# Attention values with the probabilities as the stationary operand in six of 32 head pairs, and a rank product with the last tokens on 128 rows

## The chip, the cores and the metric

The kernel runs on one core of a Trainium2 chip. The metric is the device time of one execution, in microseconds. The core has TensorE (matrix products, PE in the profile; its weight loads are a line of their own, PEld), VectorE (DVE), ScalarE (ACT), GpSimd (POOL) and SyncE (SP), which here issues the DMAs. Products go to PSUM, here in tiles of 512 float32 columns (a bank) on 128 partitions; all other data live in SBUF, on 128 partitions too.

## The reference

Eight batches, eight heads, 576 tokens, head width 64, all in float32. Causal attention with a decay is followed by a low-rank mix of the tokens and a two-layer network over the channels.

```python
def _attn_ref(q, k, v, f):
    scores = (1 / np.sqrt(D)) * np.matmul(q, k.transpose(0, 1, 3, 2))
    cum = np.cumsum(np.log(np.clip(f, 0.0001, 1.0)), axis=-1)
    scores = np.where(causal, -1e9, scores + cum[:, :, :, None] - cum[:, :, None, :])
    attn = np.exp(scores - np.max(scores, axis=-1, keepdims=True))
    attn = attn / (np.sum(attn, axis=-1, keepdims=True) + 1e-09)
    return np.matmul(attn, v)                     # 8 x 8 x 576 x 64

def _moe_ref(x, U, V, w_ch1, w_ch2):              # x: 8 x 576 x 512, heads side by side
    h = x.transpose(0, 2, 1) @ U @ V              # U 576 x 32, V 32 x 576
    u = x + h.transpose(0, 2, 1)
    return u + np.maximum(u @ w_ch1, 0.0) @ w_ch2 # 512 -> 2048 -> 512
```

## The kernel before, in words

**Tiling.** The work of attention is cut into 32 pairs of heads (`p`, four to a batch, `NP`), the 576 tokens into four chunks of 128 (`NM`, `MAIN` = 512) and a tail of 64 (`TAIL`). In most products float32 numbers are split into a high and a low part of the type float32r, and the product is made of three (or two) such products. The first six pairs (`p < NF`) instead use plain float32 operands in the score and value products; the profile shows each plain float32 product as two weight loads and two matmuls.

**Order.** `step(t)` is written out by hand for TensorE: ten slots (`s`), in which three pairs are in work at once. Pair `p = SEQ[t]` gets its scores, pair `a = SEQ[t-1]` has its probabilities turned and its first head's values made, pair `c = SEQ[t-2]` gets its second head's values, its turned result and its rank product. `SEQ` has an empty place after the fourth pair. `defer(phase, fn)` puts the ACT and DVE work that follows a product into the next slot, sorted by phase; `at(phase, fn)` does the same in the present slot. TensorE's order is as written (and SP's too in the first step and from the eighth on); that of the other engines comes from the framework's planner. In free places of the slots, and in steps of their own kind (`mix_units`), the mix and the first `NA` = 6 of 16 hidden chunks of the network run for batches that are done. After the attention, a sweep over the tokens makes the other ten chunks; it takes roughly the last 500 us and the change does not touch it.

**Probabilities and values.** A score product `score(p, j, i)` leaves rows of 128 queries; `P[j][i]` holds their exponentials, 128 queries by up to 512 keys. The 64 tail queries of both heads share one tile, `ptl`. `turn_p` and `turn_tail` turn 128 by 128 blocks with TensorE (`T`, `T_v`), and ScalarE copies them to `PTh` (for `p >= NF` VectorE makes the low part `PTl`), with one run of columns for each key chunk, at `OC`. `turn_small` turns the last 64 key columns of the tail queries to `PT4`. `values_direct` (`p < NF`) then makes the values transposed: the 128 columns of `vr` (both heads' values, a chunk of keys) are the stationary operand and up to 448 columns of `PTh` pass; half of the output rows belong to the other head and are not used. ScalarE copies the head's own 64 rows to `xT`, `turn_x` turns four blocks of `xT` back and `turn_small` the last 64 tokens, and VectorE multiplies them with the reciprocal sums `rv` into `xn`, the batch's activations.

**Rank product.** `split_x` splits a pair's 128 columns of `xn` into `xh` (ACT) and `xl` (POOL), and `ranks` multiplies them with `Us` (U's high and low parts side by side, 64 columns): four token chunks of 128 rows, and then two products on the 64 rows of the tail.

**Buffers.** `psV` has one buffer of two banks, which `T_v`, the turned tail, and both value products of a pair take in turn; `psT` has two buffers of one bank.

The helper that splits a tile:

```python
def split(dh, dl, src, heng, leng):     # heng copies to dh, leng writes src - dh to dl
```

Of the kernel before, what the change touches and what calls it, by code (L numbers as in the profile page):

```python
# [8 lines left out]
F32 = mybir.dt.float32  # L9
F32R = mybir.dt.float32r  # L10
# [3 lines left out]
ALU = mybir.AluOpType  # L14
# [7 lines left out]
P = 128  # L22
NHP = H // 2
NM = 4
# [7 lines left out]
MASKED = -8.0e9  # L32
OC = (0, 576, 1024, 1344)
PTW = 1536
NG = B + 1
NX = 3
NF = 6
# [3 lines left out]
def tile_decay_attention_moe(ctx, tc, qk, v, f, U, V, w1, w2, out):  # L41
# [6 lines left out]
    def words(ap):  # L48
        return ap.bitcast(I32)
# [140 lines left out]
    def load_w(u):  # L190
        if u in staged or u >= len(UNITS):
            return
        kind, fc = UNITS[u]
        n = {"U": (NM + 1) * RK, "V": S}.get(kind, 512)
        if kind == "w2":

            spare = xn[NX - 1].rearrange("p c d -> p (c d)").bitcast(I32)
            if fc % 2:
                raw, a = spare[:, 1536:2560], sb.tile([P, 512], I32, tag="w2a", name=f"stg{u}")
            else:  # L200
                raw, a = spare[:, 0:1024], spare[:, 1024:1536]
        else:
            t = sf.tile([P, 3 * S], I32, tag=("uh", "ul", "hh", "hl")[u % 4], name=f"stg{u}")
            raw, a = t[:, 0 : 2 * n], t[:, 2 * n : 3 * n]
        staged[u] = raw.rearrange("p (n t) -> p n t", t=2), a
        if kind == "w1":
            nc.sync.dma_start(raw, w1_src(fc))
        elif kind == "w2":
            tc.keep_in_program_order(nc.sync.dma_start(raw, w2_src(fc)))
        elif kind == "V":  # L210
            for g in range(4):
                nc.sync.dma_start(raw[32 * g : 32 * g + 32], words(V))
        else:
            r4 = raw.rearrange("p (c r) -> p c r", c=NM + 1)
            nc.gpsimd.memset(r4[64:128, NM], 0)
            nc.sync.dma_start(r4[:, 0:NM], words(U[0:MAIN]).rearrange("(c p) r -> p c r", p=P))
            nc.sync.dma_start(r4[0:64, NM], words(U[MAIN:S]))

    def decode_w(u):
        load_w(u)  # L220
# [70 lines left out]
    def make_vs(p):  # L291
        if p < NF:
            return
        vr = st[p]["vr"]
        VS = sb.tile([P, NM + 1, 2, P], F32R, tag="VS", name=f"VS{p}")
        st[p]["VS"] = VS
        for j in range(2):
            vh = VS[:, :, j, 64 * j : 64 * j + 64]
            vl = VS[:, :, j, 64 * (1 - j) : 64 * (1 - j) + 64]
            nc.scalar.copy(vh, vr[:, :, j])  # L300
            nc.gpsimd.tensor_tensor(vl, vr[:, :, j], vh.bitcast(F32), op=ALU.subtract)

    def copy(eng, dst, src, keep):
        i = eng.copy(dst, src) if eng is nc.scalar else eng.tensor_copy(dst, src)  # L304
# [104 lines left out]
    def inverse(p):  # L409
        z = st[p]  # L410
        sm = z["sm"]
        z["rv"] = sb3.tile([P, 10], F32, tag="rv", name=f"rv{p}")
        nc.vector.tensor_tensor(sm[:, 8:9], sm[:, 8:9], sm[:, 9:10], op=ALU.add)
        nc.vector.tensor_scalar(sm[:, 0:9], sm[:, 0:9], 1e-9, None, op0=ALU.add)
        nc.vector.reciprocal(z["rv"][:, 0:9], sm[:, 0:9])
        nc.vector.tensor_copy(z["rv"][0:64, 9:10], z["rv"][64:128, 8:9])

    def evac(dsth, dstl, src):
        defer(0, lambda: nc.scalar.copy(dsth, src))  # L419
        if dstl is None:  # L420
            return
        defer(2, lambda: nc.vector.tensor_tensor(dstl, src, dsth.bitcast(F32), op=ALU.subtract))  # L422
# [3 lines left out]
    def turn_p(p, j, g):  # L426
        z = st[p]
        if "PTh" not in z and p < NF:
            z["PTh"] = sb.tile([P, 2, PTW], F32, tag=("PTh", "PTl")[p % 2], name=f"PTh{p}")
            z["PT4"] = sb.tile([P, P], F32, tag="PT4", name=f"PT4{p}")  # L430
        elif "PTh" not in z:
            z["PTh"] = sb.tile([P, 2, PTW], F32R, tag="PTh", name=f"PTh{p}")
            z["PTl"] = sb.tile([P, 2, PTW], F32R, tag="PTl", name=f"PTl{p}")
            z["PT4"] = sb.tile([P, P], F32R, tag="PT4", name=f"PT4{p}")
        grp = GRP[g]
        if (j, g) == (0, 2):
            z["tv"] = psV.tile([P, 1024], F32, tag="V", name=f"T{p}_v")
            tp = z["tv"][:, 0:512]
        else:
            tp = psT.tile([P, 512], F32, tag="T", name=f"T{p}_{j}{g}")  # L440
        for x, (c, i) in enumerate(grp):
            nc.tensor.transpose(tp[:, P * x : P * x + P], z["P"][j][i][:, P * c : P * c + P], ident)  # L442

        x = 0
        for c in sorted({c for c, _ in grp}):
            m = sum(1 for cc, _ in grp if cc == c)
            sl = slice(OC[c], OC[c] + P * m)
            evac(z["PTh"][:, j, sl], z["PTl"][:, j, sl] if p >= NF else None, tp[:, P * x : P * (x + m)])
            x += m

    def turn_tail(p):
        z = st[p]
        tp = z["tv"][:, 512:1024]
        for c in range(NM):
            nc.tensor.transpose(tp[:, P * c : P * c + P], z["ptl"][:, P * c : P * c + P], ident)

        tpv = tp.rearrange("p (c j t) -> p j c t", c=NM, j=2)
        for c in range(0, NM, 2):
            o = [(OC[c + y] + MAIN - P * (c + y)) // TAIL for y in range(2)]
            pair = [  # L460
                z[n].rearrange("p j (y d) -> p j y d", d=TAIL)[:, :, o[0] : o[1] + 1 : o[1] - o[0]]
                for n in ("PTh", "PTl")
                if n in z
            ]
            evac(pair[0], pair[1] if p >= NF else None, tpv[:, :, c : c + 2])

    def turn_small(pa, px):

# [28 lines left out]

    X0 = 384

    def values_direct(p, j):  # L500


        z = st[p]
        if j == 0:
            z["xT"] = sb.tile([P, S], F32, tag="xT", name=f"xT{p}")
        vr, xT, pt = z["vr"].rearrange("p c j d -> p c (j d)"), z["xT"], z["PTh"]
        pv = psV.tile([P, 1024], F32, tag="V", name=f"V{p}_{j}")
        nc.tensor.matmul(pv[:, X0:512], vr[:, 0], pt[:, j, 0:P], start=True, stop=True)
        for c in range(NM):
            lo = max(P * c, P)  # L510
            nc.tensor.matmul(  # L511
                pv[:, X0 + lo : X0 + S], vr[:, c], pt[:, j, OC[c] + lo - P * c : OC[c] + S - P * c],
                start=c == 0, stop=False,
            )
        nc.tensor.matmul(
            pv[:, X0 + MAIN : X0 + S], vr[0:64, NM], z["PT4"][0:64, 64 * j : 64 * j + 64], start=False, stop=True
        )
        defer(1, lambda: nc.scalar.copy(xT[OWN[j]], pv[OWN[j], X0 : X0 + S]))

    def values(p, j):  # L520
        if p < NF:
# [41 lines left out]
    def split_x(p):  # L563
        z = st[p]
        X = xn[z["b"] % NX]
        fs = slice(P * z["hp"], P * z["hp"] + P)
        z["xh"] = sb.tile([P, NM + 1, P], F32R, tag="xh", name=f"xh{p}")
        z["xl"] = sb.tile([P, NM + 1, P], F32R, tag="xl", name=f"xl{p}")
        split(z["xh"], z["xl"], X[:, :, fs], nc.scalar, nc.gpsimd if p < NP - 1 else nc.vector)

    TSb = {}

    def ranks(p):
        z = st[p]
        b, hp = z["b"], z["hp"]
        if hp == 0:
            TSb[b] = sf.tile([P, DM], F32R, tag="TS", name=f"TS{b}")
        TS = TSb[b]
        fs = slice(P * hp, P * hp + P)
        tp = psT.tile([P, 512], F32, tag="T", name=f"Tt{p}")  # L580
        for i in range(NM + 1):
            kk = P if i < NM else TAIL
            for x, xx in enumerate((z["xh"], z["xl"])):
                nc.tensor.matmul(  # L584
                    tp[0:64, 0:P], Us[0:kk, i], xx[0:kk, i], start=i == 0 and x == 0, stop=i == NM and x == 1
                )


        defer(1, lambda: nc.scalar.copy(TS[0:64, fs], tp[0:64, 0:P]))
        defer(1, lambda: nc.scalar.copy(TS[96:128, fs], tp[0:32, 0:P]))  # L590
        defer(
            4,
            lambda: nc.vector.tensor_tensor(
                TS[64:96, fs], tp[0:32, 0:P], TS.bitcast(F32)[0:32, fs], op=ALU.subtract
            ),
        )
# [164 lines left out]
    def step(t):  # L761
# [11 lines left out]
        for s in range(6 + 2 if last else SLOTS):  # L773
# [9 lines left out]
                clear_operands()  # L783
            if s == 3 and pa:
                at(4, lambda: make_vs(a))
            if s == 9 and pa:
                at(4, lambda: inverse(a))
            if s == 6 and NF <= nxt_p < NP:
                at(5, lambda: parts(p + 1, 0, ENGINES))
# [28 lines left out]
                values(c, 1)  # L818
            if pa and s < 3:
                turn_p(a, 0, s)  # L820
            if px and s == (2 if last else 3):
                turn_x(c)
            if s == (3 if last else 4) and (pa or px):
                turn_small(a if pa else None, c if px else None)
            if pa and s == 5:
                turn_tail(a)
            if pa and 6 <= s < 9:
                turn_p(a, 1, s - 6)
            if pa and s == 7:
                values(a, 0)  # L830
            if px and s == (6 if last else 8):
                ranks(c)

# [344 lines left out]
```

## Time and profile before

| | |
|---|---|
| median of three runs | 1281.25 us (1280.5 to 1281.74) |
| the profiled execution | 1281.79 us, of which the span of its instructions is 1280.0 us |
| PE busy / PEld busy | 1237.0 us / 1081.7 us |
| DVE / ACT / POOL busy | 882.6 us / 654.2 us / 323.1 us |
| mean granted TensorE clock | 0.993 |

Busy times are of spans that overlap for TensorE: a matmul's span goes on while the next has begun, so what a product costs is read from start to start. A form such as `128*64 128x128` is the part of the array that is used (rows by columns) and the shape that passes. The pages cut the span into 40 slices of 32 us; the first six pairs lie between 11 us and about 170 us.

### The profile page before, as it was taken

Reading aid. Unit: us, or ns where it says so; the run is one execution under the profiler, and the core shown is the slowest. Engines: PE = TensorE matmul, PEld = TensorE weight load, DVE = VectorE, ACT = ScalarE, POOL = GpSimd, SP = SyncE. Lnnn points to the kernel's source line nnn. Section 1 sums busy time; section 2 is a strip of 40 time slices with the busy share of each in tenths; the row PEclk is TensorE's granted clock in tenths of the full one; section 3 lists DMA queues with packets and bytes.
Section 4 is the critical chain, followed back from the end, with each engine's and each line's share of the span. In section 5 each row is a group of like instructions: output and inputs, shape, how many; then the busy total and the mean of one; then the engine's idle time right before and its main releaser. Section 6 shows DMA issues by size and latency. Waiting matters only on the chain.

```text
span 1280.0 us, 21478 instructions
## 1 busy us (share of the span) xinstructions
PE 1237.0 (97%) x7644; PEld 1081.7 (85%) x7644; DVE 882.6 (69%) x2247; ACT 654.2 (51%) x1779; POOL 323.1 (25%) x306
## 2 busy tenths in 40 slices
PE   5998999999999999999999989999999999999998
PEld 3766788998998998989988878888888888888887
DVE  6666578877778668678677599985655646556453
ACT  5676777866777667778657444332122221212221
POOL 4453544444444434444433100000000000000000
PEclk9997999999999999999999999999999999999999
DMA  7334333532533524335323156110311303113010
GB/s 203 104 97 131 81 94 86 159 104 58 160 95 99 153 67 139 106 87 159 85 76 105 67 181 244 61 67 8 125 72 61 132 4 129 67 66 129 4 34 33
DMA packets 67466, 125.85 MB, mean 98 GB/s; under 512 B 7280, under 2 KB 31856, under 8 KB 65312
## 3 DMA queue, kind: packets, MB, share of 16 engines
q1 hardware_dynamic: 67232, 124.48, 31.4%
q8 instruction: 60, 0.98, 0.3%
q14 instruction: 46, 0.38, 0.1%
q10 hardware_dynamic: 128, 0.01, 0.0%
HBM read 88.67 MB, written 35.78 MB: 97 GB/s over the span
## 4 chain that ended last, share of the span: by engine, by line
PE 82%; DVE 8%; ACT 3%; issue 3%; DMA 2%; POOL 1%; SPq 0%; ACTq 0%; DVEq 0%; POOLq 0%
PE O L960 17%; PE M L1036 14%; PE A L677 10%; PE B L695 10%; PE V L534 5%; PE T L442 4%; PE S L344 3%; PE S L341 2%; PE S L345 2%; PE V L511 2%; PE Hb L946 2%; PE Tt L584 2%; DMA u<-ud 1%; PE Tx L552 1%; DVE xn L1019 1%
## 5 line engine op out<-in xcount | busy, mean ns | idle before, releaser
L1059 DVE TENSOR_TENSOR sum<-M,sum 128x256 f32<-128x256 f32 x280 | 117.7, 423 | 162.8 <-PE M L1036 159.9
L937 ACT ACTIVATE bh<-sum 128x256 fp32r<-128x256 f32 x160 | 66.3, 418 | 250.4 <-DVE sum L1059 250.4
L365 DVE CUSTOM_DVE_ANT_0 S<-S,mask 128x128 f32<-128x128 f32 (+3 forms) x256 | 126.2, 497 | 92.4 <-PE S L345 65.9
L373 ACT ACTIVATE P<-S,nm 128x128 f32<-128x128 f32 (+3 forms) x256 | 136.7, 535 | 58.7 <-DVE nm L365 57.0
L960 PE MATMUL O<-b2h,bh 128*128 128x512 f32 x360 | 143.2, 398 | 0.0
L960 PE MATMUL O<-b2l,bh 128*128 128x512 f32 x360 | 142.6, 396 | 0.0
L960 PE MATMUL O<-b2h,bl 128*128 128x512 f32 x360 | 142.0, 395 | 0.0
L677 PE MATMUL A<-uh,w1h 128*128 128x256 f32 (+1 forms) x384 | 121.1, 315 | 1.4 <-DVE hl L681 1.4
L677 PE MATMUL A<-ul,w1h 128*128 128x256 f32 (+1 forms) x384 | 113.5, 295 | 0.0
L677 PE MATMUL A<-uh,w1l 128*128 128x256 f32 (+1 forms) x384 | 113.4, 295 | 0.0
L304 POOL CAST G<-qk 64x576 fp32r<-64x576 f32 x52 | 34.3, 660 | 272.5 <-PE St L345 152.7
L695 PE MATMUL B<-w2h,hh 128*128 128x512 f32 x216 | 90.8, 420 | 2.1 <-DVE ost L709 1.4
L442 PE MATMUL T<-ident,P 128*128 128x128 f32 x544 | 89.2, 281 | 0.5 <-DVE PTl L422 0.5
L695 PE MATMUL B<-w2l,hh 128*128 128x512 f32 x216 | 85.0, 393 | 0.0
L695 PE MATMUL B<-w2h,hl 128*128 128x512 f32 x216 | 84.7, 392 | 0.0
L422 DVE TENSOR_TENSOR PTl<-T,PTh 128x512 fp32r<-128x512 f32 (+1 forms) x156 | 79.2, 529 | 5.2 <-ACT PTh L419 3.6
L960 PEld LDWEIGHTS O<-b2l,bh 128*128 128x128 f32 x360 | 67.9, 189 | 16.5
L320 POOL TENSOR_TENSOR G<-qk,G 64x576 fp32r<-64x576 f32 x52 | 74.4, 1431 | 17.0 <-ACT G L304 16.9
L960 PEld LDWEIGHTS O<-b2h,bl 128*128 128x128 f32 x360 | 68.3, 190 | 11.3
L344 PE MATMUL S<-G 128*128 128x128 f32 x208 | 72.0, 350 | 5.6 <-ACT Ptl L401 3.2
L960 PEld LDWEIGHTS O<-b2h,bh 128*128 128x128 f32 x360 | 68.3, 190 | 10.7
L938 DVE SCALAR_TENSOR_TENSOR bl<-sum,bh 128x256 fp32r<-128x256 f32 x160 | 66.5, 419 | 14.7 <-ACT bh L937 14.1
(232 smaller groups left out, 3487.1 us busy)
## 6 DMA issues: line engine op xcount, KB each, us to landing
qk<-in_qk_dram SPq DMA_DIRECT2D x104, 288.0 KB
u<-ud SPq DMA_DIRECT2D x16, 1024.0 KB
sr<-in_w_dram SPq DMA_DIRECT2D x20, 512.0 KB
vr<-in_v_dram SPq DMA_DIRECT2D x32, 256.0 KB
accd<-ost SPq DMA_DIRECT2D x32, 256.0 KB
xn<-accd SPq DMA_DIRECT2D x8, 1024.0 KB
out_dram<-xn SPq DMA_DIRECT2D x32, 256.0 KB
ud<-uh SPq DMA_DIRECT2D x7, 1024.0 KB
```

The source lines that it names most:

```text
L320: em.tensor_tensor(g[own, 1, cols], q[own], gf[own, 0, cols], op=ALU.subtract)
L344: nc.tensor.matmul(ps, G[j][:, 0, c0 : c0 + P], G[j][:, 2, cols], start=first, stop=False)
L365: nc.vector.tensor_tensor_reduce(ps[:, :w], ps[:, :w], mask[:, 512 - w : 512], scale=-SCALE, scalar=3.0e38, op0=ALU.add, op1=ALU.min, accu ...
L373: nc.scalar.activation(pt, ps[:, :w], AF.Exp, bias=z["nm"][:, col : col + 1], scale=-1.0, accum_out=z["sm"][:, col : col + 1])
L422: defer(2, lambda: nc.vector.tensor_tensor(dstl, src, dsth.bitcast(F32), op=ALU.subtract))
L442: nc.tensor.transpose(tp[:, P * x : P * x + P], z["P"][j][i][:, P * c : P * c + P], ident)
L677: nc.tensor.matmul(ps[:, :nt], wt[:, fc, c], ut[:, c, sl], start=m == 0, stop=m == 3 * NDC - 1)
L695: nc.tensor.matmul(ps, ht[:, fc, P * x : P * x + P], wt[:, fc], start=fc == 0 and m == 0, stop=fc == NA - 1 and m == 2,)
L938: nc.vector.scalar_tensor_tensor(hl, src, 0.0, hh.bitcast(F32), op0=ALU.max, op1=ALU.subtract)
L960: nc.tensor.matmul(po, ht[:, P * x : P * x + P], wt_[i], start=k == 0 and m == 0, stop=k == NB - 1 and m == 2)
L1036: nc.tensor.matmul(ps, a[x][:, c], b[y][:, c], start=m == 0, stop=m == 5)
L1059: nc.vector.tensor_tensor(dst, ps, other, op=ALU.add)
```

## The change

For `p < NF` the value product is turned round: the turned probability block (128 keys by 128 queries) is the stationary operand and the 64 value columns of the head pass, so that the result comes out with the queries on the partitions. `xT`, `turn_x` and `turn_small`'s second half fall away for these pairs, the scaling by `rv` reads the value product's PSUM, and the tail queries of both heads get a product of their own, `values_tail`, in slot 8 (`PTt` holds their turned blocks). The reciprocal sums are made in slot 6 instead of 9 for these pairs. `PTh` is filled with one copy for each group of blocks. For all 32 pairs, `ranks` multiplies the last 64 tokens in one product of 128 rows: the high parts on rows 0 to 63, the low parts on rows 64 to 127, with U's last rows loaded twice. For `p >= NF`, `make_vs` splits the values of both heads with one copy and one subtraction.

```diff
             r4 = raw.rearrange("p (c r) -> p c r", c=NM + 1)
-            nc.gpsimd.memset(r4[64:128, NM], 0)
             nc.sync.dma_start(r4[:, 0:NM], words(U[0:MAIN]).rearrange("(c p) r -> p c r", p=P))
-            nc.sync.dma_start(r4[0:64, NM], words(U[MAIN:S]))
+            for g in range(2):
+                nc.sync.dma_start(r4[64 * g : 64 * g + 64, NM], words(U[MAIN:S]))
...
-        for j in range(2):
-            vh = VS[:, :, j, 64 * j : 64 * j + 64]
-            vl = VS[:, :, j, 64 * (1 - j) : 64 * (1 - j) + 64]
-            nc.scalar.copy(vh, vr[:, :, j])
-            nc.gpsimd.tensor_tensor(vl, vr[:, :, j], vh.bitcast(F32), op=ALU.subtract)
+        halves = VS.rearrange("p c j (y d) -> p c (j y) d", y=2)
+        split(halves[:, :, 0:4:3], halves[:, :, 1:3], vr, nc.scalar, nc.gpsimd)
...
-        nc.vector.tensor_copy(z["rv"][0:64, 9:10], z["rv"][64:128, 8:9])
+        if p >= NF:
+            nc.vector.tensor_copy(z["rv"][0:64, 9:10], z["rv"][64:128, 8:9])
...
+        if p < NF:                                   # turn_p
+            o = (0, 4 * P, 7 * P)[g]
+            evac(z["PTh"][:, j, o : o + P * len(grp)], None, tp[:, 0 : P * len(grp)])
+            return
...
+        if p < NF:                                   # turn_tail
+            evac(z["PTt"], None, tp)
+            return
...
     def values_direct(p, j):
-        nc.tensor.matmul(pv[:, X0:512], vr[:, 0], pt[:, j, 0:P], start=True, stop=True)
-        for c in range(NM):
-            lo = max(P * c, P)
-            nc.tensor.matmul(
-                pv[:, X0 + lo : X0 + S], vr[:, c], pt[:, j, OC[c] + lo - P * c : OC[c] + S - P * c],
-                start=c == 0, stop=False,
-            )
-        nc.tensor.matmul(
-            pv[:, X0 + MAIN : X0 + S], vr[0:64, NM], z["PT4"][0:64, 64 * j : 64 * j + 64], start=False, stop=True
-        )
-        defer(1, lambda: nc.scalar.copy(xT[OWN[j]], pv[OWN[j], X0 : X0 + S]))
+        for i in range(NM):
+            for c in range(i + 1):
+                o = OC[c] - TAIL * c + P * (i - c)
+                nc.tensor.matmul(
+                    pv[:, D * i : D * i + D], pt[:, j, o : o + P], vr[:, c, j], start=c == 0, stop=c == i
+                )
+        def use():
+            nc.vector.tensor_tensor(dst[:, :, j], src, rv[:, :, j], op=ALU.mult)
+        defer(4, use)
+
+    def values_tail(p):
+        pv = z["pv"][:, 512 : 512 + P]
+        for c in range(NM):
+            lhs = z["PTt"][:, P * c : P * c + P]
+            nc.tensor.matmul(pv, lhs, z["vr"][:, c].rearrange("p j d -> p (j d)"), start=c == 0, stop=False)
+        nc.tensor.matmul(
+            pv, z["PT4"][0:64], z["vr"][0:64, NM].rearrange("p j d -> p (j d)"), start=False, stop=True
+        )
+        def use():
+            for j in range(2):
+                rows, cols = OWN[j], slice(D * j, D * j + D)
+                nc.vector.tensor_scalar(dst[:, cols], pv[rows, cols], z["rv"][rows, 8:9], None, op0=ALU.mult)
+        defer(4, use)
...
-        split(z["xh"], z["xl"], X[:, :, fs], nc.scalar, nc.gpsimd if p < NP - 1 else nc.vector)
+        nc.scalar.copy(xh, X[:, :, fs])
+        eng.tensor_tensor(z["xl"], X[:, 0:NM, fs], xh.bitcast(F32)[:, 0:NM], op=ALU.subtract)
+        eng.tensor_tensor(xh[64:128, NM], X[0:64, NM, fs], xh.bitcast(F32)[0:64, NM], op=ALU.subtract)
...
-            kk = P if i < NM else TAIL
-            for x, xx in enumerate((z["xh"], z["xl"])):
-                nc.tensor.matmul(
-                    tp[0:64, 0:P], Us[0:kk, i], xx[0:kk, i], start=i == 0 and x == 0, stop=i == NM and x == 1
-                )
+            for x, xx in enumerate((z["xh"], z["xl"])[: 2 if i < NM else 1]):
+                nc.tensor.matmul(tp[0:64, 0:P], Us[:, i], xx[:, i], start=i == 0 and x == 0, stop=i == NM)
...
-            if s == 9 and pa:
+            if pa and s == (9 if a >= NF else 6):
                 at(4, lambda: inverse(a))
...
-            if px and s == (2 if last else 3):
+            if px and c >= NF and s == (2 if last else 3):
                 turn_x(c)
...
+            if pa and a < NF and s == 8:
+                values_tail(a)
             if px and s == (6 if last else 8):
                 ranks(c)
```

More of the change, by code (lines that the diff above doesn't have):

```diff
@@ L34 @@
 PTW = 1536
+PTJ = PTW - NM * TAIL
 NG = B + 1
@@ L428, in turn_p @@
         if "PTh" not in z and p < NF:
-            z["PTh"] = sb.tile([P, 2, PTW], F32, tag=("PTh", "PTl")[p % 2], name=f"PTh{p}")
+            t = sb.tile([P, 2 * PTW], F32, tag=("PTh", "PTl")[p % 2], name=f"PTh{p}")
+            z["PTh"], z["PTt"] = t[:, 0 : 2 * PTJ].rearrange("p (j w) -> p j w", j=2), t[:, 2 * PTJ :]
             z["PT4"] = sb.tile([P, P], F32, tag="PT4", name=f"PT4{p}")
@@ L447, in turn_p @@
             sl = slice(OC[c], OC[c] + P * m)
-            evac(z["PTh"][:, j, sl], z["PTl"][:, j, sl] if p >= NF else None, tp[:, P * x : P * (x + m)])
+            evac(z["PTh"][:, j, sl], z["PTl"][:, j, sl], tp[:, P * x : P * (x + m)])
             x += m
@@ L462, in turn_tail @@
                 for n in ("PTh", "PTl")
-                if n in z
             ]
-            evac(pair[0], pair[1] if p >= NF else None, tpv[:, :, c : c + 2])
+            evac(pair[0], pair[1], tpv[:, :, c : c + 2])
     def turn_small(pa, px):
@@ L498, in tile_decay_attention_moe, with x_out @@
     X0 = 384
+    def x_out(p):
+        z = st[p]
+        fs = slice(P * z["hp"], P * z["hp"] + P)
+        X = xn[z["b"] % NX]
+        rv = z["rv"][:, 0:8].rearrange("p (i j) -> p i j", j=2).unsqueeze(3).broadcast_to([P, NM, 2, D])
+        return X[:, 0:NM, fs].rearrange("p i (j d) -> p i j d", j=2), rv, X[0:64, NM, fs]
     def values_direct(p, j):
         z = st[p]
-        if j == 0:
-            z["xT"] = sb.tile([P, S], F32, tag="xT", name=f"xT{p}")
-        vr, xT, pt = z["vr"].rearrange("p c j d -> p c (j d)"), z["xT"], z["PTh"]
@@ L507, in values_direct @@
-        pv = psV.tile([P, 1024], F32, tag="V", name=f"V{p}_{j}")
-        nc.tensor.matmul(pv[:, X0:512], vr[:, 0], pt[:, j, 0:P], start=True, stop=True)
-        for c in range(NM):
-            lo = max(P * c, P)
-            nc.tensor.matmul(
-                pv[:, X0 + lo : X0 + S], vr[:, c], pt[:, j, OC[c] + lo - P * c : OC[c] + S - P * c],
-                start=c == 0, stop=False,
-            )
+        vr, pt = z["vr"], z["PTh"]
+        z["pv"] = pv = psV.tile([P, 1024], F32, tag="V", name=f"V{p}_{j}")
@@ new lines, in values_direct @@
+        for i in range(NM):
[4 more added lines that the diff above has]
+                )
+        src = pv[:, 0 : NM * D].rearrange("p (i d) -> p i d", i=NM)
+        def use():
+            dst, rv, _ = x_out(p)
+            nc.vector.tensor_tensor(dst[:, :, j], src, rv[:, :, j], op=ALU.mult)
+        defer(4, use)
@@ L515, in values_direct @@
+    def values_tail(p):
+        z = st[p]
+        pv = z["pv"][:, 512 : 512 + P]
+        for c in range(NM):
+            lhs = z["PTt"][:, P * c : P * c + P]
+            nc.tensor.matmul(pv, lhs, z["vr"][:, c].rearrange("p j d -> p (j d)"), start=c == 0, stop=False)
         nc.tensor.matmul(
-            pv[:, X0 + MAIN : X0 + S], vr[0:64, NM], z["PT4"][0:64, 64 * j : 64 * j + 64], start=False, stop=True
+            pv, z["PT4"][0:64], z["vr"][0:64, NM].rearrange("p j d -> p (j d)"), start=False, stop=True
@@ L517, in values_direct @@
         )
-        defer(1, lambda: nc.scalar.copy(xT[OWN[j]], pv[OWN[j], X0 : X0 + S]))
+        def use():
+            dst = x_out(p)[2]
+            for j in range(2):
+                rows, cols = OWN[j], slice(D * j, D * j + D)
+                nc.vector.tensor_scalar(dst[:, cols], pv[rows, cols], z["rv"][rows, 8:9], None, op0=ALU.mult)
+        defer(4, use)
     def values(p, j):
@@ L567, in split_x @@
         z["xh"] = sb.tile([P, NM + 1, P], F32R, tag="xh", name=f"xh{p}")
-        z["xl"] = sb.tile([P, NM + 1, P], F32R, tag="xl", name=f"xl{p}")
-        split(z["xh"], z["xl"], X[:, :, fs], nc.scalar, nc.gpsimd if p < NP - 1 else nc.vector)
+        z["xl"] = sb.tile([P, NM, P], F32R, tag="xl", name=f"xl{p}")
+        xh, eng = z["xh"], nc.gpsimd if p < NP - 1 else nc.vector
+        nc.scalar.copy(xh, X[:, :, fs])
+        eng.tensor_tensor(z["xl"], X[:, 0:NM, fs], xh.bitcast(F32)[:, 0:NM], op=ALU.subtract)
+        eng.tensor_tensor(xh[64:128, NM], X[0:64, NM, fs], xh.bitcast(F32)[0:64, NM], op=ALU.subtract)
     TSb = {}
@@ L820, in step @@
                 turn_p(a, 0, s)
-            if px and s == (2 if last else 3):
+            if px and c >= NF and s == (2 if last else 3):
                 turn_x(c)
-            if s == (3 if last else 4) and (pa or px):
-                turn_small(a if pa else None, c if px else None)
+            if s == (3 if last else 4) and (pa or (px and c >= NF)):
+                turn_small(a if pa else None, c if px and c >= NF else None)
             if pa and s == 5:
```

## The prediction

> **What bounds the kernel now.** I read the page from the top: busy shares, slices, chain; then busy time by stretches of the attention; then TensorE's timeline in one step.
>
> ```profile
> PE 1237.0 (97%) x7644; PEld 1081.7 (85%) x7644; DVE 882.6 (69%) x2247; ACT 654.2 (51%) x1779; POOL 323.1 (25%) x306
> PE   5998999999999999999999989999999999999998
> PEclk9997999999999999999999999999999999999999
> PE 82%; DVE 8%; ACT 3%; issue 3%; DMA 2%; POOL 1%; SPq 0%; ACTq 0%; DVEq 0%; POOLq 0%
> 48.00:100.00 52.00, 50.50 (x267) 35.40 (x265) 35.84 (x94) 38.41 (x109) 24.44 (x28) 1.00 0.31 95
> 200.00:300.00 100.00, 97.79 (x655) 89.23 (x653) 75.44 (x208) 71.82 (x204) 46.00 (x40) 1.00 0.38 109
> ```
>
> The columns of the last two rows are the stretch, its length, then busy time of PE, PEld, DVE, ACT, POOL, and the granted clock. In the first pairs (48 to 100 us) and in the split pairs (200 to 300) PE has work 97 to 98% of the time and no other engine passes 76%: the order written out for PE is the path. So a nanosecond that leaves PE's list is a nanosecond of the kernel, as long as no wait takes its place. The one dent in the clock is in the fourth slice.
>
> **A step of the first pairs.** PE's timeline (start, length, count of matmuls):
>
> ```profile
> 62.18 0.39 PE L508 MATMUL V<-PTh,vr 128*128 128x128 f32 x2
> 62.40 2.53 PE L511 MATMUL V<-PTh,vr 128*128 128x448 f32 x8
> 64.86 0.43 PE L515 MATMUL V<-PT,vr 64*128 64x64 f32 x2
> 65.22 0.66 PE L442 MATMUL T<-ident,P 128*128 128x128 f32 x4
> 67.46 1.02 PE L341 MATMUL S<-qk 68*128 68x512 f32 x2
> 68.32 0.60 PE L552 MATMUL Tx<-ident,xT 128*128 128x128 f32 x4
> 68.76 1.14 PE L341 MATMUL St<-qk 68*128 68x288 f32 x4
> 53.08 0.27 PE L473 MATMUL Ty<-ident,xT 128*64 128x128 f32 x1
> 53.19 1.14 PE L341 MATMUL St<-qk 68*128 68x288 f32 x4
> ```
>
> *Removed.* One head's values run from 62.18 to 65.22; the four turnings after them take 0.66 instead of the 0.60 of those at 68.32, so they really begin 0.06 later: 3.10 us a head. `turn_x` costs 68.76 - 68.32 = 0.44, the turning of the last 64 tokens 53.19 - 53.08 = 0.11.
>
> *Added, values.* Ten products a head, each plain float32, so 20 matmuls, each with its own load of 128 columns, and 64 passing columns. Passing costs 0.43 us for 512 columns (67.46 to 68.32, two matmuls), 0.84 ns a column, so 54 ns for 64. The load is the larger part. What a load of 128 columns costs shows where small products follow one another:
>
> ```profile
> 304.13 0.19 PEld L345 LDWEIGHTS S<-G 128*128 128x128 f32 x1
> 304.24 0.19 PEld L531 LDWEIGHTS V<-PTh,VS 128*128 128x128 f32 x1
> 304.35 0.71 PEld L534 LDWEIGHTS V<-PTh,VS 128*128 128x128 f32 x4
> 304.18 0.28 PE L345 MATMUL S<-G 128*128 128x128 f32 x1
> 304.30 0.27 PE L531 MATMUL V<-PTh,VS 128*128 128x128 f32 x1
> ```
>
> Loads start 0.11 us apart, and so do the two matmuls, though their 128 split columns alone pass in about half that (0.06, the full-row step of the rank product below). Bounds for the new matmul: 54 ns if loads hid entirely, 54 + 109 = 163 ns if load and passing took turns. I take 109 ns, the load alone, since these rows show loads running under the matmul before them, and the plain float32 pair at 62.18 shows the same 0.22 for two. A head: 20 x 0.109 = 2.18 us (bounds 1.08 and 3.26), 0.92 less than now, 1.84 a pair.
>
> *Added, `values_tail`.* Eight full matmuls like those at 62.18: 0.88 us. Then one product on 64 rows, as at 64.86: that block now takes from about 64.77 (the eight matmuls of L511 pass 2816 columns, 2.37 us, after 62.40) to 65.28, 0.51; with 64 more columns 0.57. Together 1.45 us a pair.
>
> *Rank product, all 32 pairs.* The matmuls on 64 rows stand apart from their neighbours:
>
> ```profile
> 385.36 0.22 PE L584 MATMUL Tt<-xh,Us 128*64 128x128 f32 x1
> 385.41 0.22 PE L584 MATMUL Tt<-xl,Us 128*64 128x128 f32 x1
> 385.57 0.27 PE L584 MATMUL Tt<-xh,Us 64*64 64x128 f32 x1
> 385.68 0.22 PE L584 MATMUL Tt<-xl,Us 64*64 64x128 f32 x1
> 385.83 0.50 PE L695 MATMUL B<-w2h,hh 128*128 128x512 f32 x1
> 386.17 0.40 PE L695 MATMUL B<-w2h,hl 128*128 128x512 f32 x1
> L584 PEld LDWEIGHTS Tt<-xl,Us 64*64 64x64 f32 x32 | 4.3, 136 | 0.0
> ```
>
> From 385.41 to 386.17 are 0.76 us. With one product of 128 rows there stand instead 0.06 (the step between full-row ones, first two rows), a load of 0.11 and the 0.23 of a 512-column product (386.17 less 385.83 less its late start): 0.40. That saves 0.36 us a pair. Bounds: 0.11 (only the second product goes) and 0.41.
>
> *Other engines.*
>
> ```profile
> L518 ACT COPY xT<-V 64x576 f32<-64x576 f32 x12 | 7.6, 635 | 10.9 <-PE V L515 10.9
> L554 DVE TENSOR_TENSOR xn<-Tx,rv 128x512 f32<-128x512 f32 x32 | 21.9, 684 | 2.6 <-PE Tx L552 2.6
> L489 DVE TENSOR_TENSOR xn<-Ty,rv 64x128 f32<-64x128 f32 x30 | 8.5, 282 | 0.4
> L177 POOL TENSOR_TENSOR xl<-xn,xh 128x640 fp32r<-128x640 f32 x31 | 48.9, 1578 | 19.9 <-ACT xh L174 19.2
> L71 POOL TENSOR_TENSOR Us<-stg,Us 128x160 fp32r<-128x160 f32 x1 | 0.5, 521 | 0.0
>   PEld Tt L584: 0.4, 1
> ```
>
> ACT loses two copies of 635 ns a first pair and three fixed costs of merged copies. DVE loses 684 + 282 and gets two scalings of 256 columns and two of 64: between the 684 of the same elements in one and about twice that; ACT at 38.41 and DVE at 35.84 of 52 us cover it, so I cost it at nothing; without that cover it is at most 0.7 us a pair. POOL's second subtraction in `split_x` costs up to 0.5 us (the 128x160 row), while the first falls by a fifth of 1578; the last row says that PE waited only once, 0.4 us, for `xl` in the whole run, so this hides as well. `make_vs` becomes one POOL instruction like the 1578 row instead of two of half its size. The inverse moves three slots ahead on DVE, behind exponentials that are two slots old by then; queued behind it is only the new scaling that needs it. U's rows are loaded once more by SP and POOL loses a clearing, once, long before their use.
>
> *A new wait?* `psV` has one buffer. The second head's values wait for DVE's scaling of the tail (before: for ACT's 635 ns copy, a slot earlier). Behind the tail product PE still has a rank product and two score products, about 1.9 us, against two short DVE instructions; the same for `T_v` behind the second head's scaling. I take no wait.
>
> **The clock.** PE's clock is not constant at the start. Scores at 34 us take twice as long as those at 68.76, and later stretches show the granted clock (second to last but two column):
>
> ```profile
> 34.21 2.13 PE L341 MATMUL St<-qk 68*128 68x288 f32 x4
> 36.13 1.06 PE L455 MATMUL T_v<-ident,Ptl 128*128 128x128 f32 x4
> 37.84 1.49 PE L341 MATMUL S<-qk 68*128 68x128 f32 x4
> 39.76 0.63 PE L508 MATMUL V<-PTh,vr 128*128 128x128 f32 x2
> 98.71:102.11 3.40, 2.20 (x15) 1.30 (x13) 3.40 (x12) 2.75 (x9) 1.54 (x1) 1.00 0.30 92
> 102.12:105.52 3.40, 3.40 (x12) 2.14 (x11) 3.33 (x7) 2.10 (x7) 2.56 (x2) 0.50 0.27 83
> 112.36:115.77 3.41, 3.41 (x11) 2.26 (x10) 1.31 (x3) 1.70 (x5) 0.00 (x0) 0.50 0.00 0
> ```
>
> The half clock of 102.12 to 115.77 is four windows of 3.41 us, and on that grid a window ends at 40.68, where the first values go from half to full speed. PE's rows from 34.21 on follow one another without a gap, so being busy was not enough. Weighing passing columns by the rows they use (scores 68 of 128), the window 33.86 to 37.27 comes to 0.72 of its time and did not lift the clock; 37.27 to 40.68, with 0.92 us of full-row values, comes to 0.82 and did. In the new form these values pass only half the time (54 of 109 ns): 0.69. I therefore expect the clock to stay halved at 40.68, through the next window (new values alone, 0.5), and to rise after the third at 47.5, when turnings and the tail's full matmuls give about 0.83. Two windows at half clock lose 6.8 x 0.5 = 3.4 us. Bounds: nothing, and all windows to about 80 us, 19.7.
>
> The Trainium skill, "TensorE: Matmul & The Clock Gate", Part 1, says that the clock is halved by default and that about 3.4 us of sustained activity lift it; the 13.65 us above agree with its window. It does not say what counts as activity; if busy instructions did, 40.68 would stay and the sum would lack the 3.4.
>
> **The sum** (us). First pairs: -1.84 + 1.45 - 0.44 - 0.11 - 0.36 = -1.30, by six: -7.8. The 26 others: 26 x 0.36 = 9.4; a tenth of it, in steps where PE waits anyway, is lost: -8.4. Around the empty place in the order (81 to 104 us) PE already waits for ACT and turns less; there I give back 1.0. Clock: +3.4. Together -11.8, from 1281.79 (span 1280.0) to 1270.0; the median of the runs stands 0.54 below the profiled execution, so 1269.5.
>
> **Rivals.**
> (a) *The clock rises at 40.68 as before.* For it: nothing in a row shows that the weighing by rows is right. Time 1269.5 - 3.4 = 1266.
> (b) *Waits take the place.* VectorE at 75.44 of 100 and PE's stops at ScalarE's exponentials would swallow half the rank gain and more of the first pairs': 4 to 7 us, 1275; against it, 98% PE. If all of both went, no change.
> (c) *The clock stays halved for long* (the other side). Place: 40.68 on. Without the clock the sum is -15.2, and each window at half clock gives back 1.7; from nine windows, to 71 us, it decides. Up to 80 us: +19.7, 1285.5. For it: the new values take 4.3 us each at half clock and keep the array half empty. Against it: the third window above is at 0.83, past the 0.82 that sufficed.
> (d) *Load and passing take turns*, 163 ns: 12 heads x 1.08 = +13.0, and in the tail 6 x 8 x 0.109 = +5.2, so -15.2 + 18.2 = +3.0: about 1284. Against it stand the loads at 304 us, 0.11 apart. The Trainium skill has this on the same page, Part 3, "What overlaps and what doesn't": a load overlaps running matmuls only where row groups differ. Those rows, all on 128 rows, disagree.
>
> **Chances.** Forecast 0.46; (a) 0.21; (b) 0.17 for a part and 0.05 for all; (c) 0.07; (d) 0.04. 0.2% of the time, 2.6 us, is about what a measurement can tell from no change. Faster by more: 0.46 + 0.21 + 0.16 = 0.83; within: 0.06; slower: 0.11. The range leaves out (c), (d) and the loss of all: 1264 (case (a) with hidden-load gains) to 1278.
>
> **What would show it.** New value matmuls 0.109 us apart, 2.2 us a head; `turn_x` gone for six pairs and a step of about 9.4 us; the rank product's last three gaps 0.36 shorter in each pair; the granted clock full from 47.5; no new waits on VectorE before the value products. Wrong would make it: 0.16 between those matmuls, half clock past 60 us, or PE idle before `V` or `Tt`.

## The result, and the profile after

The changed kernel takes 1263.78 us (median of four runs, 1260.36 to 1277.08) against 1280.88 for the kernel before: 0.989 of its time, 95% interval 0.9859 to 0.992. The forecast was 1269.5, range 1264 to 1278: the median lies 0.2 us under the lower end of the range, and so do two of the four single runs (1260.36 and 1260.68). The profiled execution takes 1266.87 us, its span is 1265.0. The page:

```profile
PE 1218.7 (96%) x7738; PEld 1083.4 (86%) x7738; DVE 883.9 (70%) x2254; ACT 643.3 (51%) x1723; POOL 325.4 (26%) x310
PEclk9999999999999999999999999999999999999999
PE 79%; DVE 12%; ACT 4%; issue 3%; DMA 2%; POOL 0%; SPq 0%; ACTq 0%; DVEq 0%; POOLq 0%
```

TensorE stays the path; 18 us of its busy time are gone, and so is the dent in the clock's fourth slice. TensorE's timeline in the changed kernel, start and length in us, then the count:

```profile
36.57 1.06 PE L461 MATMUL T_v<-ident,Ptl 128*128 128x128 f32 x4
40.20 4.37 PE L525 MATMUL V<-vr,PTh 128*128 128x64 f32 x20
44.36 1.59 PE L340 MATMUL S<-qk 68*128 68x384 f32 x2
48.74 1.35 PE L340 MATMUL S<-qk 68*128 68x512 f32 x4
49.92 2.34 PE L525 MATMUL V<-vr,PTh 128*128 128x64 f32 x20
52.10 0.61 PE L444 MATMUL T<-ident,P 128*128 128x128 f32 x4
59.07 2.34 PE L525 MATMUL V<-vr,PTh 128*128 128x64 f32 x20
375.44 0.23 PE L622 MATMUL Tt<-xl,Us 128*64 128x128 f32 x1
375.51 0.22 PE L622 MATMUL Tt<-xh,Us 128*64 128x128 f32 x1
375.85 0.40 PE L731 MATMUL B<-w2h,hl 128*128 128x512 f32 x1
```

A head's values take 52.10 - 49.92 = 2.18 us, as forecast (20 x 0.109). The second head's values of one pair and the first head's of the next begin 9.15 us apart; before it was 10.61. The difference, 1.46, is one head (0.92) and the two turnings (0.55) of the forecast. The rank product's end, from the last low product on 128 rows to the second 512-column product, takes 0.41 us (375.44 to 375.85), before 0.76. And the first values, at 40.20, still run at half clock: 4.16 us for what later takes 2.18. The trace's record of the granted clock has the first rise at 48.45 us; the forecast was 47.5.

How much was gained where is read from the last product of `ranks` for the sixth and for the last pair, before and after:

```profile
170.71 0.22 PE L584 MATMUL Tt<-xl,Us 64*64 64x128 f32 x1
731.09 0.21 PE L584 MATMUL Tt<-xl,Us 64*64 64x128 f32 x1
```
```profile
163.88 0.22 PE L622 MATMUL Tt<-xh,Us 128*64 128x128 f32 x1
715.83 0.22 PE L622 MATMUL Tt<-xh,Us 128*64 128x128 f32 x1
```

| us | forecast | measured in the profiled executions |
|---|---|---|
| to the end of the sixth pair | -7.8 + 1.0 + 3.4 = -3.4 | 163.88 - 170.71 = -6.8 |
| the 26 split pairs | -8.4 | 551.95 - 560.38 = -8.4 |
| the sweep | 0 | +0.3 |
| span | -11.8 | -15.0 |

### The profile page after: what moved, and what is told of

The parts are those of the page before. It is cut to its first block, busy times and chain, and to the rows that moved or that the text cites. A ratio compares the mean times of both kernels' runs of the same rounds, so it can differ in the third digit from the quotient of the medians.

```text
span 1265.0 us, 21657 instructions
## 1 busy us (share of the span) xinstructions
PE 1218.7 (96%) x7738; PEld 1083.4 (86%) x7738; DVE 883.9 (70%) x2254; ACT 643.3 (51%) x1723; POOL 325.4 (26%) x310
## 4 chain that ended last, share of the span: by engine, by line
PE 79%; DVE 12%; ACT 4%; issue 3%; DMA 2%; POOL 0%; SPq 0%; ACTq 0%; DVEq 0%; POOLq 0%
PE O L998 17%; PE M L1074 14%; PE A L713 10%; PE B L731 9%; PE V L569 5%; PE T L444 3%; PE S L343 3%; PE Hb L984 2%; PE S L340 2%; PE S L344 2%; PE V L525 2%; DMA u<-ud 1%; PE Tt L622 1%; DVE xn L1057 1%; PE St L340 1%
```

## The experiments

All times are medians; each kernel's ratio is to the kernel before on the same chip. An edit is told against the kernel that the sentence names.

**The parts.** First the rank product alone (the kernel before with the hunks of U's load, `split_x` and `ranks`):

> The kernel before with nothing changed but the rank product (the last tokens in one product of 128 rows; U's last rows loaded twice). Theory (a product on 64 rows drains TensorE's array, and TensorE's list is the path in all 32 pairs): about 0.35 us a pair where TensorE never waits, less where it does; in the changed kernel the 26 split pairs together gained 8.4 us, so 8.4 + 6 x 0.3 = 10 us less than before, about 1271, and the runs lie as close together as those of before, since the first pairs' clock is not touched. Rival (the gain of the split pairs comes from the values' split in one go, which frees ScalarE and GpSimd): under 3 us less than before.

Measured: 1270.5 us (1269.93 to 1272.25), ratio 0.9921 (0.9908 to 0.9933), 10.4 us less. The theory's 10 us hold and the rival's 3 are out: three fifths of the whole gain come from one small product in each pair. In the profile, counted as in the table above, the 26 split pairs take 551.83 us, 8.6 less than before, and the first six pairs 1.7 less; another 1.1 come from the sweep, where the kernel before lost the clock for a window (at 853.05) and this execution did not. Next the turned values without it (those three hunks undone in the changed kernel):

> The changed kernel with the old rank product (64-row products, U's rows cleared). Theory: the first six pairs save 6 x 0.94 = 5.6 us on TensorE's list, less 3.4 for the later rise of the clock and 1 for waits, so -1 us on average against before, 1280; single runs differ by the clock: a halved clock between 80 and 120 us costs or saves up to 7 us, so runs spread from about 1273 to 1290. Rival (the first pairs carry most of the gain): 10 us less than before.

Measured: 1273.33 us (1270.85 to 1286.22), ratio 0.995 (0.993 to 0.9969), 7.6 us less. That is more than the theory's 1 and less than the rival's 10; the spread was as expected. With a mean clock of 1.0 the runs took 1270.9 to 1271.4, at 0.988 1286.2. The two runs at about the mean clock of the kernel before (0.993 and 0.994) took 1279.66 and 1275.41, 1.2 and 5.5 us less than it. So the clock decides on most of this part's gain, and what TensorE's list alone gives cannot be read from these times. The two parts add up to 18.0, against 17 together.

**The split of the values.** The old `make_vs` in the changed kernel:

> The changed kernel with the old split of the values (two copies, two subtractions in each of the 26 split pairs). Theory: ScalarE and GpSimd have room there (72 and 46 of 100 us busy), so same time as the changed kernel within its spread, 1262 to 1264. Rival (the split in one go carries part of the gain): 2 to 8 us more.

Measured: 1261.87 us (1260.29 to 1274.53), ratio 0.9874 (0.9844 to 0.9904). In its profile the 26 split pairs take 551.37 us, in the changed kernel's two profiles 551.95 and 551.42. The split in one go carries no part of the gain that these runs could show.

**What spaces the new matmuls.** The changed kernel, with both heads' columns passing:

```diff
-  pv[:, D * i : D * i + D], pt[:, j, o : o + P], vr[:, c, j]
+  pv[:, P * i : P * i + P], pt[:, j, o : o + P], vr[:, c].rearrange("p j d -> p (j d)")
...
-  src = pv[:, 0 : NM * D].rearrange("p (i d) -> p i d", i=NM)
+  src = pv[:, 0 : NM * P].rearrange("p (i j d) -> p i j d", i=NM, j=2)[:, :, j]
```

> The changed kernel, but in the first six pairs' value products both heads' 128 value columns pass, instead of the head's own 64; the other half of the result is not read. Twice the passing columns in 240 matmuls. Theory (the load of the 128 stationary columns, 0.109 us, sets the spacing): the spacing stays 0.109 to 0.113 us at full clock, so the list grows by under 1 us; and the value products fill the array all the time, so that the window in which they begin (about 40 to 44 us) counts as full and the clock rises one or two windows earlier, 1.7 to 3.4 us less than the changed kernel, with less spread. Rival 1 (passing columns set the spacing): 240 x 0.054 = 13 us more. Rival 2 (load and passing take turns): also 13 us more. Rival for the clock (any busy matmul counts alike): first rise unmoved.

Measured: 1262.83 us (1262.46 to 1271.11), ratio 0.9867 (0.9847 to 0.9887). TensorE's timeline of this kernel:

```profile
45.18 2.40 PE L525 MATMUL V<-vr,PTh 128*128 128x128 f32 x20
54.37 2.40 PE L525 MATMUL V<-vr,PTh 128*128 128x128 f32 x20
57.58 1.06 PE L543 MATMUL V<-vr,PTh 128*128 128x128 f32 x8
```

Twice the columns in 2.40 instead of 2.34 us a head, and no 13 us more: the spacing is 112 ns in the median in both kernels, for the matmuls and for their loads of 128 stationary columns. Both rivals are out. A fixed cost of each matmul could give the same 112 ns, since no run changed the number of stationary columns; against it, the rank product's matmuls (split ones, 128 columns passing), with 64 of them, follow at 0.06 us. The part on the clock stays open: the clock rose at 38.60 us in this execution, but the window that lifted it (35.19 to 38.60) holds scores and turnings alone, and in one execution of the changed kernel itself it rose at 38.15 (next run).

**The changed kernel again.**

> The changed kernel once more, beside the others on the same chip. If the grid of 3.41 us windows lies anew against the kernel's start in each execution, single runs spread over some 15 us as in the first four (1260.4 to 1277.1), with the granted clock lower where the time is longer: 0.014 of mean clock lost is about 35 us at half speed, 17 us. If the spread came from something else, time and clock would not go together.

Measured: 1263.98 us (1261.14 to 1276.11), ratio 0.9888 (0.9852 to 0.9924). Single runs with their mean clock: 1261.1 (0.999), 1262.2 (0.997), 1262.5 (0.999), 1265.4 (1.0), 1274.4 (0.986), 1276.1 (0.986). The two long runs have the low clock, as expected. The 1265.4 at 1.0 does not fit; the mean clock leaves out the time before the first rise (last section), and a late first rise costs time too: the kernel with the old split, whose clock first rose at 49.77 us in its profile, took 1267.66 there at a mean of 0.998. No profile fell on one of the two long runs, so where they lost the clock was not seen. The profiled one shows what the grid does:

```profile
36.31 1.06 PE L461 MATMUL T_v<-ident,Ptl 128*128 128x128 f32 x4
38.02 0.89 PE L340 MATMUL S<-qk 68*128 68x128 f32 x4
38.74 0.49 PE L444 MATMUL T<-ident,P 128*128 128x128 f32 x3
39.07 2.34 PE L525 MATMUL V<-vr,PTh 128*128 128x64 f32 x20
```

The same program, 0.26 us ahead of the first profile at the turnings of the tail (36.31, 36.57), and nearly the same grid: a window ends at 38.15 here, at 38.21 there. Here the clock rises at its end, and the first values begin at full speed. Weighed as in the forecast, this window was full to 0.77 here and to 0.76 there, where it did not lift the clock. By this weighing, 0.01 decides on ten microseconds at half speed: the first pair's rank product ends at 59.15 here, at 64.22 there, 5.1 us for 10.3 us less at half clock.

**Do rows count?** The changed kernel with the scores of the first six pairs over all 128 rows:

```diff
-  nc.gpsimd.memset(t[0:68, z0 : z0 + 64], 0.0)
+  nc.gpsimd.memset(t[64:128], 0.0)
+  nc.gpsimd.memset(t[0:64, z0 : z0 + 64], 0.0)
...
-  nc.tensor.matmul(ps, q[0:68, c0 : c0 + P], k[0:68, cols], ...)
+  nc.tensor.matmul(ps, q[:, c0 : c0 + P], k[:, cols], ...)
```

> The changed kernel, but the first six pairs' score products run over all 128 rows: rows 68 to 127 of q and k are zeros, cleared by GpSimd at each load. Same columns, same loads, same results; only the rows in use grow from 68 to 128. Theory (the clock's windows count passing columns weighted by the rows in use): the scores that begin at 11 us fill the window from about 14 to 18 us completely, so the clock first rises at 14 to 22 us instead of 38 to 48; scores, turnings and first values to 40 us then take half as long where VectorE and ScalarE keep up, 3 to 8 us less than the changed kernel's usual 1262, less a us for GpSimd's clearing; it may fall back to half where TensorE waits. Rival (rows do not count, or zeros do not count as work): first rise at 35 to 48 us as before, time 1262 to 1264 or a little more.

Measured: 1263.28 us (1261.52 to 1265.2), ratio 0.9864 (0.985 to 0.9878). The first pair's tail scores, before and in this kernel, and a wait of the latter:

```profile
15.70 4.05 PE L341 MATMUL St<-qk 68*128 68x288 f32 x8
```
```profile
15.99 2.10 PE L341 MATMUL St<-qk 128*128 128x288 f32 x8
34.87 1.30 PE L341 MATMUL St<-qk 128*128 128x288 f32 x2 [7.48 <-POOL stg L70]
31.00 0.48 SPq L330 DMA_DIRECT2D qk<-cumd  x1
```

With rows of zeros added, and nothing else but their clearing, the same eight matmuls run at full speed: the clock first rises at 15.76 us. In all eight profiles with 68-row scores (the kernel before, the changed kernel twice, and the kernels of five experiments) it rose between 38.1 and 49.8. So rows in use count, zeros or not, and the rival is out. The time did not follow: TensorE now stood 7.48 us before the second pair's tail scores, whose decay rows SyncE issued only at 31.00, and in that wait the clock fell to half again, from 29.41 to 39.65. (The row puts the wait down to a GpSimd instruction that ended just then; the last experiment names the rows.) The half clock had hidden a late transfer.

Both edits together:

> The changed kernel with both: score products of the first six pairs over 128 rows (60 of zeros), and both heads' 128 value columns passing. Theory: every product of the first pairs then fills the array, no window without a wait of over half its length falls under the 0.37 at which the clock was lost, and slow single runs (1274 to 1277 in the changed kernel) become rarer; median at or under that of the padded scores alone. Rival: as that run, with the same spread.

Measured: 1262.63 us (1261.69 to 1264.55), ratio 0.9861 (0.9848 to 0.9874), first rise at 14.72. None of the four runs is a long one, but the padded kernel had none either (at most 1265.2): the runs don't tell the two apart.

**The wait that was not foreseen.** In the changed kernel TensorE waits before the tail's product:

```profile
78.10 1.16 PE L542 MATMUL V<-vr,PTh 128*128 128x128 f32 x8 [0.17 <-DVE xn L532]
91.71 1.16 PE L542 MATMUL V<-vr,PTh 128*128 128x128 f32 x8 [1.09 <-DVE xn L532]
93.21 0.27 PE L622 MATMUL Tt<-xh,Us 128*64 128x128 f32 x1
```

`xn` L532 is VectorE's scaling of the first head's values, in the other bank of the same tile. It takes 0.42 us, but at 91.23 VectorE came to it from other work. With a tile of its own:

```diff
-  pv = z["pv"][:, 512 : 512 + P]
+  pv = psT.tile([P, 512], F32, tag="T", name=f"Vt{p}")[:, 0:P]
```

> The changed kernel, but the tail queries' product takes a PSUM tile of its own (from the turned blocks' two buffers) instead of the second bank of the first head's values. In the changed kernel TensorE stands before that product until VectorE has scaled the first head's values: 1.09 us in the step without scores, 0.17 us in one other. Theory (the wait goes with the shared tile): those waits go, about 1 us less than the changed kernel, not more than a measurement can tell; rival: the tile now waits for ScalarE's copies of turned blocks or delays the rank product by as much, same time.

Measured: 1261.42 us (1259.73 to 1266.28), ratio 0.9856 (0.9839 to 0.9873). Its timeline:

```profile
85.75 0.27 PE L444 MATMUL T<-ident,P 128*128 128x128 f32 x1
85.86 1.06 PE L542 MATMUL Vt<-vr,PTh 128*128 128x128 f32 x8
87.26 0.27 PE L622 MATMUL Tt<-xh,Us 128*64 128x128 f32 x1
```

The wait is gone and nothing took its place. Between the last rank products of the first and the second pair lie 15.48 us instead of 15.92 (before the change 16.76, 1.28 more: the 1.30 a pair of the forecast), between those of the second and the third 12.25 instead of 13.60 (before the change 13.05, so that with the shared tile this step had become longer). In the times of whole runs this is within the spread.

**Towards a better version.** With the own tile, the first pair's scores alone over 128 rows:

> The tail product in its own tile, and score products over 128 rows (60 of zeros) for the first pair alone, whose rows are cleared before anything runs. Theory (rows count for the clock; after that the decay rows of the second pair, issued by SyncE at about 30 us, are the next limit): first rise at 14 to 18 us, then TensorE idles before the second pair's tail scores until about 33 to 35 us, where it stood at half clock before; the clock may fall in that idle time. So only 0 to 2 us less than the kernel with the own tile alone (1261.4). Rival (the clock alone sets the first 40 us): 6 us less or more.

Measured: 1264.19 us (1260.99 to 1268.78), ratio 0.9878 (0.986 to 0.9897), no gain. The clock rose at 16.27 us, fell at 23.09, in TensorE's wait of 2.70 us for ScalarE, and came back at 40.16. The rival is out. Last, the first two pairs padded, and V's loads moved behind the decay rows on SyncE's queue:

```diff
-  steps = [lambda: load_w(u + (3 if u < 6 else 2)), lambda: decode_w(u)]
+  steps = [lambda: u == 2 or load_w(u + (3 if u < 6 else 2)), lambda: decode_w(u)]
...
   place_decay(1, 1, cumd)
+  load_w(5)
```

> As that, with the scores of the first two pairs over 128 rows, and with V's four loads moved on SyncE's queue behind the second pair's second head and its decay rows, which stood behind them. Theory (those rows are the limit once the clock is up): they land 2 to 4 us earlier, TensorE's idle time before the second pair's tail scores (7.5 us with all scores padded) shrinks by as much, and the time is 2 to 5 us under the kernel with the own tile, 1257 to 1260. Rival (another transfer or VectorE's work on weights comes next): same time as without the move.

Measured: 1257.69 us (1257.15 to 1258.47), ratio 0.9817 (0.9805 to 0.983): under both kernels, with an interval apart from the changed kernel's. SyncE's queue and TensorE in it:

```profile
25.69 0.48 SPq L333 DMA_DIRECT2D qk<-cumd  x1
27.32 3.15 SPq L213 DMA_DIRECT2D stg<-in_V_dram  x4
32.09 0.78 PE L345 MATMUL St<-qk 128*128 128x288 f32 x2 [2.75 <-DMA qk<-cumd]
37.27 2.34 PE L530 MATMUL V<-vr,PTh 128*128 128x64 f32 x20
```

Against the kernel with all scores padded, the decay rows go out at 25.69 instead of 31.00 and the wait shrinks from 7.48 to 2.75 us; against the changed kernel, the first values begin at 37.27, at full clock, instead of 40.20 at half clock. In two waits the clock still fell for a window, at 22.38 and at 32.62. This kernel makes two edits at once, the second pair's padding and the move, and no run has the one without the other: that the rows go out earlier and the wait ends sooner is shown, how much of the time the move alone gives is not, and so its rival was not tested.

## Why the prediction was right, and where it was not

Right, each by its row: the price of the new matmul (the load, 0.109; measured 0.112), the tail product (1.45; 87.26 - 85.86 = 1.40 where nothing holds it up), the turnings, the 0.36 of the rank product (0.35), and that TensorE's order is the path: of 26 x 0.35 = 9.1 us in the split pairs 8.4 arrived. Of the rivals, load and passing taking turns (d) is shown wrong by the doubled columns. The clock halved for long (c) did not come: the latest first rise in any profile is at 49.77. (By its own terms, 1269.5 - 3.4 + 19.7, its 1285.5 should read 1285.8.) Of the waits of (b), 4 to 7 us, some 2.5 came, all in the first pairs.

The step on the clock was right as a mechanism and right in the profiled execution: the window that lifted the clock was full to 0.82 (forecast 0.83), and the half clock cost about the 3.4 us. The first pair's rank product ends 3.38 us later than before, 64.22 against 60.84 us; 0.44 of it is a later start (the tail's turnings at 36.57 instead of 36.13) and -0.6 the list's gain up to there (three heads at -0.92, two tails at +1.45, the turnings at -0.55 and part of the rank product, -0.2), which leaves 3.6 for the clock.

But I took the first rise as settled by the program. It is not: in the second profile of the same kernel a window 0.06 us earlier was full enough, and the first values met the full clock, as in rival (a); and between the kernel before and the one with the rank product alone, which start alike, the grid lay 1.1 us apart (rises at 40.68 and 39.58). The five profiles with the new values and scores on 68 rows (the changed kernel twice, and those with the old rank product, the old split and the own tile) have the first rise at 38.15, 39.98, 41.00, 48.45 and 49.77: late in two of five. So 3.4 is not a term of the sum but one of its values, and that the execution profiled with the result was a late one was luck. Five of the changed kernel's ten runs took 1260.4 to 1262.5, under (a)'s 1266 by part of what follows.

Two terms were missed. "I take no wait" was wrong, and with it came one of the forecast's own signs of being wrong, TensorE idle before `V`: I asked who waits for the buffer's release and not who waits inside it. The tail's product shares a tile with the first head's values and stood behind their scaling, 0.44 us in one step and 1.35 in the next by the own-tile run, 1.8 in the two (of them 0.17 and 1.09 as idle time). The 1.0 given back around the empty place was a guess of about the right size: TensorE's waits for ScalarE's `PTh` there grew from 0.97 (0.50 and 0.47) to 1.64 us.

And the sum left the half clock of 102 to 116 us as it was. Of 17 runs of the kernel before beside the first experiments, 16 have a mean clock of 0.993 (one 0.995), as four such windows and one later make it; the changed kernel's runs mostly have 0.997 to 1.0. From the fourth pair's last rank product to the fifth's it takes 42.59 us instead of 47.81. Of these 5.2 us TensorE's list gives 0.8 (three heads at -0.92, two tails at +1.45, one pair's turnings and rank product at -0.91), so by subtraction some 4.4 come from the clock. It goes with the turned values: the rank product alone has the same four windows at half clock (101.02 to 114.67), the turned values alone have none. TensorE's wait there became shorter, 1.20 us for ScalarE's `Ptl` before and with the rank product alone, 0.66 in the changed kernel and 0.74 with the turned values alone.

```profile
101.71 0.91 PE L340 MATMUL S<-qk 68*128 68x384 f32 x2 [0.66 <-ACT Ptl L400]
99.65:103.05 3.40, 2.74 (x20) 1.86 (x18) 3.31 (x13) 2.40 (x10) 0.81 (x3) 1.00 0.32 93
103.06:106.47 3.41, 2.41 (x12) 1.25 (x10) 3.32 (x10) 3.02 (x9) 2.09 (x2) 1.00 0.44 141
```

TensorE is busy 2.74 of 3.40 us in the window of that wait, where it was 2.20 before, and the clock holds. That ScalarE's two missing copies made the wait shorter is argued, not shown; and in the second profile of the same kernel, where a window ends elsewhere, the clock did fall there (busy 2.10 of 3.41 us), for one window instead of four. The runs with a mean clock of 0.986 stay unexplained.

Put together, the first six pairs come to -7.8 (list) + 0.4 (start) + 3.6 (clock at the start) + 1.8 (tail's wait) + 0.7 (`PTh`) - 0.5 (`Ptl`) - 4.4 (clock at 102 us) = -6.2, where -6.8 was measured and -3.4 forecast. The missed terms have both signs, so the forecast came as near as it did in part by luck.

One figure was misnamed: the "step of about 9.4 us" is the stretch between two value products (9.15), not ten slots, which take 15.92 from one pair's rank product to the next's.

## What to carry to other kernels

Look for products that use a part of the array's rows, however small: here 64 such matmuls, with the gaps around them, cost 10 us of 1281 more than 32 on full rows, and the low parts fit on the idle rows. In these runs a plain float32 product with few passing columns took the time of its loads, and TensorE's clock went by how full the array's rows were in fixed stretches of 3.41 us: price a rewrite near the start, or near a stall, with both clocks. Where a faster stage gains nothing, look at the transfer that the slow one had hidden, and ask of every shared buffer who waits inside it.

## What the runs showed of the hardware that was not expected

- TensorE at half clock was busy without a gap and stayed there: in the profiles of the two kernels compared, windows full to 0.53, 0.65, 0.71 and 0.76 by rows and columns did not lift it, 0.82 did; rows of zeros lifted it at 15 us. The same weighing over every window of all twelve profiles (an estimate from starts and shapes, at 0.84 ns for a plain column and half of it for a split one, twice that at half clock, good to about 0.02) separates nearly all: the clock rose after windows of 0.77 and more and stayed halved after 0.76 and less (one at 0.77); it was lost after 0.39 and less and kept after 0.38 and more. Without the rows, windows busy all the time stand on both sides. Turnings count in full: the windows that lifted the clock at 38.15 and 38.60 hold only them and scores.
- The Trainium skill ("TensorE: Matmul & The Clock Gate", Part 1) gives the window of 3413 ns, free-running against the kernel; the runs agree: first rises and falls lie whole windows apart within an execution (in the changed kernel 48.45 and 836.93, 231 windows), and its place against the kernel's start differs between executions.
- The view of busy times shows a granted clock of 1.00 before the first recorded change, where the matmuls' own lengths (4.05 against 2.10 us for the same eight) say half.
